# Strassen's scheme in the first product of the second MLP, with the planner's order kept to the end

## The chip, the cores and the metric

The kernel runs on one core of a Trainium2 chip. TensorE (PE) multiplies, VectorE (DVE), ScalarE (ACT) and GpSimd (POOL) work on elements, and SyncE (SP) issues most of the transfers, in the order of its queue. The metric is the device time of one execution in microseconds, the median of several.

## What is computed

An attention block feeds two MLPs one after the other; the tokens are 2304, the model width is 512 and the inner width 2048. The second MLP is the one that changes:

```python
def _moe2_ref(x, w_in, w_out, a, b):
    h = x @ w_in                       # 2304x512 by 512x2048: the first product
    h2 = h * h
    h3 = h2 * h
    P = a[0] + a[1] * h + a[2] * h2 + a[3] * h3
    Q = 1.0 + np.abs(b[0]) * np.abs(h) + np.abs(b[1]) * h2
    g = P / (Q + 1e-06)
    return (g @ w_out)                 # 2304x2048 by 2048x512: the second product
```

## The kernel before

**Split operands.** Every MLP operand is held as a rounded part and a rest (hi and lo, ACT's copy and a subtraction), and each block of a product is three matmuls into one PSUM bank: hi by hi, hi by lo, lo by hi.

**Tiles and units.** The second MLP goes through the tokens in six tiles of 384 (`T2`). Inner columns are taken 128 at a time, `ff` 0 to 15; a pair of tile and `ff` is a unit. `stage_a` makes the first product of a unit: four blocks of the model width, 12 matmuls of 128x384 (L1039 to L1041), into a bank `h` or `at`. `stage1`, `stage2` and `stage3` make the rational function of it on ACT, DVE and POOL and split the result into `gh` and `gl`. `stage_b`, three units later, makes the second product: three token blocks of 128, 9 matmuls of 128x512 (L1082 to L1084), into three banks `acc`. So a unit has 21 matmuls. `split_x` splits the tile's input, which `load_y` fetches.

**Weights.** During the last two tiles of the first MLP, `conv2_a` and `conv2_b` turn the weights of the second MLP from 64-bit into 32-bit floats and split them, one half of an `ff` at a time (half 0 is `w_in`, half 1 is `w_out`). They then stay in SBUF for all six tiles; those of `ff` 12 to 15 go out to HBM for a while and come back in `reload2`.

**Order.** A planner in the kernel (`plan`) simulates the engines with fixed costs and lists each engine's instructions in order. Its list is made binding for instructions that it starts before 600 us of its own clock (the last argument at the call); behind that the framework's scheduler keeps the written order, changed by priorities.

Of the kernel before, what the change touches and what calls it, by code (L numbers as in the profile page):

```python
# [8 lines left out]
F32 = mybir.dt.float32  # L9
# [50 lines left out]
SHARED = {("two", "wide"): 0.7, ("two", "thin"): 0.25, ("one", "wide"): 0.7, ("one", "thin"): 0.3,  # L60
          ("wide", "two"): 0.2, ("wide", "one"): 0.05, ("thin", "two"): 0.6, ("thin", "one"): 0.3}
HOLD, ROUNDS = 0.0, 6
DMA_RATE, DMA_LATENCY, LANES = 320e3, 1.9, 8


# [266 lines left out]
def moe_chain_kernel(ctx, tc, qk0, v0, qk, vv, s0, s, w1, w2, ab, out):  # L332
# [6 lines left out]
    l_d = [[dr.tile([128, 512], F32, name=f"l_d{t}_{i}") for i in range(2)] for t in range(NF)]  # L339
    w2_d = {(ff, half): [dr.tile([128, 512], F32, name=f"w2_d{ff}_{half}_{i}") for i in range(2)]  # L340
            for ff in range(FS, NF) for half in range(2)}
    y_d = {a: dr.tile([128, KD, b - a], F32, name=f"y_d{a}") for a, b in zip(CUTS, CUTS[1:])}

    def t_w(name, shape, dt):
# [42 lines left out]


    pt_h, pt_l, pt_p = [], [], []
    x_t = {}  # L390
    v_t = {}
    raw_t = {}
# [280 lines left out]
    def t1(p):  # L673
        if p.pv_plain:
            if not pt_p:
                pt_p.append(sb.tile([128, 2, 960], F32, name="pt"))
# [148 lines left out]
    n = 0  # L825
# [107 lines left out]
        if T == 0:  # L933
            li_t[1, ff, half] = l

    c2_open = []

    def conv2_a(ff, half):
        c2_open.append((ff, half, conv_t(1, ff, half)))

    def conv2_b():
        ff, half, t = c2_open.pop(0)
        if ff >= FS:
            hi, lo = (tmp_tile("PA", 3, (128, 512), F32R) for _ in range(2))
        else:
            hi, lo = home2(ff, half)
        last = {i.engine: i for i in traced()}
        k0 = len(nc.cur_bb.bb.instructions)
        conv_hl(t, hi, lo)
        queue_behind({nc.scalar.engine: last[nc.scalar.engine]}, k0)  # L950
        if ff >= FS:
            for d, t in zip(w2_d[ff, half], (hi, lo)):
                nc.sync.dma_start(out=d, in_=f(t))
        else:
            w2_t[ff, half] = (hi, lo)

    def home2(ff, half):
        if ff >= 14:
            return t_l("w2h", [128, 512], F32R), t_l("w2l", [128, 512], F32R)
        if ff < 2 and ff not in w2_t:  # L960
            t = t_j("w2", [128, 2, 1024], F32R)
            w2_t[ff] = (t[:, 0], t[:, 1])
        if ff not in w2_t:
            al = t_q if ff < 5 else t_v if ff < 6 else t_w
            w2_t[ff] = (al("w2h", [128, 1024], F32R), al("w2l", [128, 1024], F32R))
        return tuple(t[:, half * 512:(half + 1) * 512] for t in w2_t[ff])

    def reload2(ff):
        for half in range(2):
# [57 lines left out]
    def stage_a_(u):  # L1027
        ph, T, ff = u
        bk = bank(hsel(ph, T, ff))
        n = TILES[ph][T][1]  # L1030
        h = bk[:, 0:n]
        if ph == 0:
            wh, wl = w1_t[ff][:, 0:512], li_t.pop((T, ff, 0))
        else:
            wh, wl = w2_t[ff, 0]
        for k in range(KD):
            xh, xl = xs_t[ph, T, k]
            cs = slice(k * 128, (k + 1) * 128)
            nc.tensor.matmul(h, wh[:, cs], xh, start=(k == 0), stop=False)  # L1039
# [48 lines left out]
    def evacuate(ph, T, acc):  # L1088
# [42 lines left out]
    def stage1_(u):  # L1131
# [23 lines left out]
    def stage2(u):  # L1155
        ph, T, ff = u
        if ph == 0:
            return
        a, t, w = e_t[u]
        c = 1.0 + 1.0e-6  # L1160
# [5 lines left out]
        e_t[u] = t  # L1166

    def stage3(u):
        with early(P_ST3):
# [13 lines left out]
    if True:  # L1183
# [76 lines left out]
        units += [(ph, T, ff) for ph in range(2) for T in range(2 - 2 * ph, 6) for ff in range(NF)]  # L1260
        NU = len(units)
        T1A = [(1, ff) for ff in range(HF)]
        c2 = [(ff, half) for r in (range(6), range(FS, NF), range(6, FS)) for ff in r for half in range(2)]
        c2_done, c2_load = [0], [0]

        def load2_to(n):
# [32 lines left out]
            return bank("at")  # L1299

        open_acc(0, 0)
        for i in range(NU + LAGS[1]):
            at_bank[0] = second_bank if i < HF + LAGS[0] else at_only
            u = units[i] if i < NU else None
            region[0] = 0 if i < 32 else 1 if i < 96 else 2
            if u is not None:
# [4 lines left out]
                gap(i, 0)  # L1311
                stage1(u)
                with ahead(C2_OFF):
                    while c2_open:
                        conv2_b()
# [29 lines left out]
            if u is not None:  # L1345
# [5 lines left out]
                if 0 < t4 <= 20:  # L1351
                    conv2_to(t4)
                elif t4 > 20:
                    ready = 6 + (t4 - 18) // 2
                    conv2_to(min(2 * (NF - FS + ready), t4, 32))
                if t4 >= 34 and t4 % 2 == 0 and FS + (t4 - 34) // 2 < NF:
                    reload2(FS + (t4 - 34) // 2)
                if ph == 0 and T == 3 and ff == 8:
                    nc.sync.dma_start(out=abt, in_=ab)
                    nc.vector.memset(qc, 1.0 + 1.0e-6)  # L1360
# [4 lines left out]
                if ph == 1 and ff == 5 and T + 1 < 6:  # L1365
                    load_y(T + 1)
# [62 lines left out]
```

## Time and profile before

| | |
|---|---|
| median of three runs | 1037.35 us (1037.16 to 1037.57) |
| span of the profiled execution | 1033.6 us; the trace gives no other time of that execution |
| busy share of the span | PE 98%, ACT 77%, DVE 76%, POOL 43% |
| granted TensorE clock | 1.00 in all slices, which is 2.4 GHz |
| second MLP on PE | from 615.72 us to about 1029.4 us |

A matmul's time from start to end includes what overlaps with its neighbours, so the price of one is the distance from its start to the next one's. Busy times of the other engines are unions.

### The profile page before, as it was taken

How to read it: one execution, taken by the hardware profiler on the slowest of the kernel's cores; microseconds unless marked ns; L12 is line 12 of the kernel's file. 1: busy time of each engine (PE TensorE's matmuls, PEld its weight loads, DVE VectorE, ACT ScalarE, POOL GpSimd, SP SyncE). 2: the span in 40 equal slices, each digit the busy share in tenths (PEclk: the TensorE clock that was granted, in tenths of full speed). 3: DMA queues.
4: the chain of work that ended last, by engine and by line, in shares of the span. 5: the costliest groups of instructions: out<-in, count | busy, mean ns of one | idle time of the engine just before them, and what ended most of it. 6: DMA issues, size and time to landing. Idle time of an engine off the chain costs nothing.

```text
span 1033.6 us, 17441 instructions
## 1 busy us (share of the span) xinstructions
PE 1011.0 (98%) x5684; PEld 917.0 (89%) x5684; DVE 785.7 (76%) x1826; ACT 791.2 (77%) x1661; POOL 448.1 (43%) x491
## 2 busy tenths in 40 slices
PE   6999999999999999999999999999999999999998
PEld 5889999889998888988999999989999999999996
DVE  5788986887987888787675887687686766877765
ACT  5998878877987777766566558778887887877875
POOL 2757664412221122223435765445444454444542
PEclk9999999999999999999999999999999999999999
DMA  9877576665564644436779855010010110100100
GB/s 249 296 241 254 186 222 195 207 187 151 161 196 131 200 147 142 139 97 215 237 228 323 303 153 189 1 31 32 1 62 1 31 31 2 56 6 1 31 1 31
DMA packets 67946, 138.66 MB, mean 134 GB/s; under 512 B 8336, under 2 KB 21456, under 8 KB 67856
## 3 DMA queue, kind: packets, MB, share of 16 engines
q1 hardware_dynamic: 65312, 133.39, 40.7%
q10 hardware_dynamic: 2544, 4.16, 1.6%
q8 instruction: 45, 0.74, 0.3%
q14 instruction: 45, 0.37, 0.1%
HBM read 110.82 MB, written 22.61 MB: 129 GB/s over the span
## 4 chain that ended last, share of the span: by engine, by line
PE 76%; DVE 9%; ACT 5%; DMA 4%; POOL 4%; issue 3%; SPq 1%; POOLq 0%; DVEq 0%; ACTq 0%
PE h L1039 7%; PE h L1040 7%; PE h L1041 7%; PE at L754 6%; PE acc L1082 5%; PE acc L1084 5%; PE acc L1083 5%; PE acc L1077 4%; PE acc L1075 4%; PE acc L1076 4%; PE at L1039 3%; PE at L1040 3%; PE at L1041 3%; PE at L614 3%; PE at L615 2%
## 5 line engine op out<-in xcount | busy, mean ns | idle before, releaser
L607 POOL TENSOR_SCALAR PA<-PA,stat 128x384 f32<-128x384 f32 (+3 forms) x112 | 72.9, 657 | 165.1 <-DVE stat L606 65.7
L1039 PE MATMUL h<-xs,w1h 128*128 128x448 f32 (+1 forms) x360 | 122.8, 342 | 1.6 <-DVE e L1141 1.5
L1040 PE MATMUL h<-xs,w1h 128*128 128x448 f32 (+1 forms) x360 | 122.6, 341 | 0.0
L1041 PE MATMUL h<-xs,w1l 128*128 128x448 f32 (+1 forms) x360 | 122.3, 340 | 0.0
L1076 PE MATMUL acc<-gl,w1h 128*128 128x448 f32 (+1 forms) x352 | 118.8, 339 | 1.2 <-POOL gl L1179 1.2
L1077 PE MATMUL acc<-gh,w1l 128*128 128x448 f32 (+1 forms) x352 | 118.8, 340 | 0.4 <-DMA w1l<-l_d 0.3
L1075 PE MATMUL acc<-gh,w1h 128*128 128x448 f32 (+1 forms) x352 | 118.4, 340 | 0.0
L1179 POOL TENSOR_TENSOR gl<-PA,gh 128x384 fp32r<-128x384 f32 x95 | 97.1, 1022 | 7.3 <-ACT gh L1177 5.0
L1082 PE MATMUL acc<-w2h,gh 128*128 128x512 f32 x252 | 99.6, 395 | 0.1
L1084 PE MATMUL acc<-w2h,gl 128*128 128x512 f32 x252 | 99.3, 394 | 0.0
L1083 PE MATMUL acc<-w2l,gh 128*128 128x512 f32 x252 | 99.2, 394 | 0.0
L1150 POOL TENSOR_TENSOR tc<-tc,e 128x384 f32<-128x384 f32 x47 | 51.2, 1089 | 97.5 <-ACT tc L1148 97.5
L604 ACT ACTIVATE PA<-PA,stat 128x384 f32<-128x384 f32 (+3 forms) x112 | 63.9, 571 | 16.4 <-DVE stat L587 14.3
L1039 PEld LDWEIGHTS h<-xs,w1h 128*128 128x128 f32 x360 | 67.9, 189 | 5.7 <-DVE e L1141 2.4
L1040 PEld LDWEIGHTS h<-xs,w1h 128*128 128x128 f32 x360 | 67.8, 188 | 3.7 <-DVE xs L1009 0.4
L1041 PEld LDWEIGHTS h<-xs,w1l 128*128 128x128 f32 x360 | 67.8, 189 | 3.2
L1076 PEld LDWEIGHTS acc<-gl,w1h 128*128 128x128 f32 x352 | 66.1, 189 | 4.6 <-POOL gl L1179 1.4
L1077 PEld LDWEIGHTS acc<-gh,w1l 128*128 128x128 f32 x352 | 66.1, 189 | 3.9 <-DMA w1l<-l_d 0.5
L1137 ACT ACTIVATE e<-h 128x448 f32<-128x448 f32 (+1 forms) x90 | 43.4, 483 | 33.5 <-PE h L1041 31.6
L1075 PEld LDWEIGHTS acc<-gh,w1h 128*128 128x128 f32 x352 | 66.1, 189 | 3.2
L1177 ACT ACTIVATE gh<-PA 128x384 fp32r<-128x384 f32 x96 | 50.4, 525 | 20.9 <-DVE PA L1165 17.7
L1163 DVE SCALAR_TENSOR_TENSOR tc<-tc,e 128x384 f32<-128x384 f32 x48 | 27.5, 574 | 51.0 <-ACT e L1162 47.9
(265 smaller groups left out, 3183.8 us busy)
## 6 DMA issues: line engine op xcount, KB each, us to landing
w1l<-l_d SPq DMA_DIRECT2D x138, 256.0 KB
raw<-in_w_dram SPq DMA_DIRECT2D x48, 512.0 KB
raw<-in_qk_dram SPq DMA_DIRECT2D x24, 384.0 KB
l_d<-w1l SPq DMA_DIRECT2D x32, 256.0 KB
raw64x<-in_w_dram SPq DMA_DIRECT2D x16, 512.0 KB
raw<-in_qk_dram SPq DMA_DIRECT2D x8, 576.0 KB
w_d<-PA SPq DMA_DIRECT2D x16, 256.0 KB
R<-in_vv_dram SPq DMA_DIRECT2D x12, 320.0 KB
```

The source lines that it names most:

```text
L604: nc.scalar.activation(pt[:, 0:n], pt[:, 0:n], AF.Exp, bias=mn, scale=-1.0, accum_out=stat[:, i, 1:2])
L607: nc.gpsimd.tensor_scalar(pt[:, 0:n], pt[:, 0:n], stat[:, i, 2:3], 1.0, op0=ALU.mult, op1=ALU.mult)
L1039: nc.tensor.matmul(h, wh[:, cs], xh, start=(k == 0), stop=False)
L1040: nc.tensor.matmul(h, wh[:, cs], xl, start=False, stop=False)
L1041: nc.tensor.matmul(h, wl[:, cs], xh, start=False, stop=(k == KD - 1))
L1075: nc.tensor.matmul(o, wh[:, cs], gh, start=first and not both, stop=False)
L1076: nc.tensor.matmul(o, wh[:, cs], gl, start=False, stop=False)
L1077: nc.tensor.matmul(o, wl[:, cs], gh, start=False, stop=last and (not both or m % 2 == 1))
L1082: nc.tensor.matmul(acc[m], gh[:, cs], wh, start=first, stop=False)
L1083: nc.tensor.matmul(acc[m], gh[:, cs], wl, start=False, stop=False)
L1084: nc.tensor.matmul(acc[m], gl[:, cs], wh, start=False, stop=last)
L1179: eng.tensor_tensor(gl, g, f(gh), op=ALU.subtract)
```

## The change

Tile sizes of the second MLP become 384, 512, 512, 512, 384. The two tiles of 384 keep the old units. The three of 512 work in four groups `q` each. A group is a product of 512 inner columns by 512 tokens: the weight `a` is cut into 2x2 blocks (256 of the inner columns by 256 of the model width, two separate pairs `p` of 128 columns) and the input `b` into 2x2 blocks (256 of the model width by 256 tokens). In place of the eight block products, seven "slots" are computed (`SLOTS`), some of them on sums and differences. A slot is 12 matmuls of 128x256 (L1336). Partial sums stay in their PSUM banks and further slots add to them; ACT copies three states of them to the SBUF tile `pt` (`save`), and DVE adds those copies back (`add`), so that four blocks of 256 inner columns by 256 tokens come out. Each goes through `act1`, `act2`, `act3` and `out_part`, whose two calls are 12 matmuls of 128x512 (L1274 to L1276).

The sums of weights are made once, in `sum_make` (four DVE operations of 128x256 for a pair of `ff`) and `sum_split` (two ACT copies, two POOL subtractions), during the conversion. All `w_in` operands go to HBM (`keep_a` and `sum_split`), and one transfer of 512 KB per slot brings them back, up to 12 slots ahead (`load_wa`). The sums of inputs are made for each tile (`operand_steps`: five DVE subtractions, seven splits on ACT and POOL). The order of the weight conversions changes. The planner's list is binding to the end.

```diff
-T2 = [(t * 384, 384) for t in range(6)]
+T2 = [(0, 384)] + [(384 + t * 512, 512) for t in range(3)] + [(1920, 384)]
+SLOTS = [("a11", "b11"), ("a12", "b21"), ("s2", "t2"), ("s1", "t1"), ("s3", "t3"), ("s4", "b22"), ("a22", "t4")]
+    def sum_make(q, p):
+        t0, t1, u = pairs[q, p]
+        a, b = slice(0, 256), slice(256, 512)
+        nc.vector.tensor_tensor(u[:, a], t1[:, a], t1[:, b], op=ALU.add)
+        nc.vector.tensor_tensor(u[:, b], t0[:, a], t1[:, a], op=ALU.subtract)
+        nc.vector.tensor_tensor(t0[:, a], u[:, a], t0[:, a], op=ALU.subtract)
+        nc.vector.tensor_tensor(t0[:, b], t0[:, b], t0[:, a], op=ALU.subtract)
...
+        nc.scalar.activation(g[:, :, 0], t, AF.Copy)
+        nc.gpsimd.tensor_tensor(g[:, :, 1], t, f(g[:, :, 0]), op=ALU.subtract)
...
+    def act2(bl):
+        r = bl.h
+        t, w, a = bl.g
+        nc.scalar.activation(a, w, AF.Ln, bias=qc)
+        nc.scalar.activation(r, a, AF.Exp, scale=-1.0)
+        nc.vector.scalar_tensor_tensor(w, w, QC, r, op0=ALU.add, op1=ALU.mult)
+        nc.vector.scalar_tensor_tensor(w, w, -2.0, r, op0=ALU.add, op1=ALU.mult)
+        nc.vector.scalar_tensor_tensor(t, t, nega[:, 0:1], w, op0=ALU.add, op1=ALU.mult)
...
+    def keep_a(ff):
+        q, p, i = ff // 4, ff // 2 % 2, ff % 2
+        dst = wa_d[q][i][:, p].rearrange("p (b h c) -> p b h c", b=2, h=2)
+        for h, t in enumerate(w2_t[ff, 0]):
+            nc.sync.dma_start(out=dst[:, :, h], in_=f(t).rearrange("p (b c) -> p b c", b=2))
+
+    def slot(T, q, a, b, o, first):
+        w, (xh, xl) = wa_t[T, q, a], ops_t[T, b]
+        for p in range(2):
+            for k in range(2):
+                cs = slice(k * 128, k * 128 + 128)
+                wh, wl = w[:, p, 0, cs], w[:, p, 1, cs]
+                for n, (x, z) in enumerate(((wh, xh), (wh, xl), (wl, xh))):
+                    nc.tensor.matmul(o[:, p * 256:p * 256 + 256], x, z[:, k], start=first and p == k == n == 0,
+                                     stop=(k, n) == (1, 2), skip_group_check=True)
+        used[0] += 1
+        load_wa(used[0] + WA_AHEAD)
...
+        def save(k, n):
+            return lambda: nc.scalar.activation(hbuf(n), st[k], AF.Copy)
+
+        def add(x, k, n, new=False):
+            def run():
+                bl[x].h = bank(tags["w"]) if new else st[k]
+                nc.vector.tensor_tensor(bl[x].h, st[k], hbuf(n), op=ALU.add)
+            return run
...
+        ev = [(1, mm(0, "z", True)), (1.1, save("z", 0)),
+              (2, mm(1, "y", True)), (2.1, add((0, 0), "y", 0)),
+              (3, mm(2, "z")), (3.1, save("z", 2)),
+              (4, mm(3, "v", True)), (4.1, save("v", 1)),
+              (5, mm(4, "z")), (5.1, add((1, 1), "z", 1, True)),
+              (6, mm(5, "v")), (6.1, add((0, 1), "v", 2)),
+              (7, mm(6, "z")), (7.1, direct)]
...
-    for line in plan(nc.cur_bb.bb.instructions, tied, 600.0):
+    for line in plan(nc.cur_bb.bb.instructions, tied, UNTIL):
```

**The order on PE in the middle of a tile.** Before, in a tile of 384 (`xs` and `yt` the input, `w2h` and `w2l` the weights):

```order
L1039 MATMUL h<-xs,w2h 128x384
L1082 MATMUL acc<-w2h,gh 128x512
L1040 MATMUL h<-xs,w2h 128x384
L1083 MATMUL acc<-w2l,gh 128x512
L1041 MATMUL h<-xs,w2l 128x384
L1084 MATMUL acc<-w2h,gl 128x512
```

Now, in the second of the tiles of 512 (`at` is the bank `z`, `h` the banks `y`, `v` and `w`; `xl` and `xs` the inputs, `wa` the slot's weights, `w2b` those of the second product):

```order
L1336 MATMUL at<-xl,wa 128x256 x12
L1274 MATMUL acc<-w2b,gh 128x512
L1275 MATMUL acc<-w2b,gh 128x512
L1276 MATMUL acc<-w2b,gl 128x512
...
L1336 MATMUL h<-xl,wa 128x256 x12
L1336 MATMUL at<-xl,wa 128x256 x12
L1274 MATMUL acc<-w2b,gh 128x512
L1275 MATMUL acc<-w2b,gh 128x512
L1276 MATMUL acc<-w2b,gl 128x512
...
L1336 MATMUL h<-xs,wa 128x256 x12
```

The two products no longer alternate one by one: slots of 12 stand between stretches of 6 or 12 matmuls of the second product, and the third slot, which adds to the bank of the first, follows the second directly.

**The order on PE where the first tile of 512 begins.** The part now, just ahead of its first second product (before, a tile's first units simply took up the same alternation):

```order
L1140 MATMUL acc<-w2b,gl 128x512 x3
L1336 MATMUL h<-xs,wa 128x256 x8
L1336 MATMUL at<-xl,wa 128x256 x5
L1336 MATMUL at<-xs,wa 128x256
L1336 MATMUL at<-xl,wa 128x256
L1336 MATMUL at<-xs,wa 128x256 x4
L1336 MATMUL h<-xs,wa 128x256
L1336 MATMUL at<-xs,wa 128x256 x7
L1336 MATMUL h<-xs,wa 128x256
L1336 MATMUL at<-xl,wa 128x256
L1336 MATMUL h<-xs,wa 128x256 x10
L1336 MATMUL at<-xl,wa 128x256 x11
```

Behind the last matmuls of the tile of 384 (L1140) only slots stand for a while, and those of the second group (`at<-xl`) are drawn in among those of the first.

**The order on POOL in the last tile of the first MLP** (`gl` is the unit's own work, `raw` and `w2l` or `w2a` the conversion). Before:

```order
L1179 TENSOR_TENSOR gl<-e,gh 128x448
L904 TENSOR_SCALAR raw64x<-raw64x 128x512
L912 TENSOR_TENSOR w2l<-tc,w2h 128x512
L1179 TENSOR_TENSOR gl<-e,gh 128x448
```

Now (`pt` are the sums' rests):

```order
L1393 TENSOR_TENSOR gl<-e,gh 128x448
L914 TENSOR_SCALAR raw64x<-raw64x 128x512
L922 TENSOR_TENSOR w2a<-tc,w2a 128x512 x2
L1393 TENSOR_TENSOR gl<-e,gh 128x448
L998 TENSOR_TENSOR pt<-tc,pt 128x2x256 x2
L922 TENSOR_TENSOR w2a<-tc,w2a 128x512
L1393 TENSOR_TENSOR gl<-e,gh 128x448
```

Between two units' `gl` there are now up to three operations of the conversion and the sums, and the last of these stand in the first tile of the second MLP.

## Rows read from the trace of the kernel before

**Rows 1.** The page's busy times of the engines.

```profile
PE 1011.0 (98%) x5684; PEld 917.0 (89%) x5684; DVE 785.7 (76%) x1826; ACT 791.2 (77%) x1661; POOL 448.1 (43%) x491
```

**Rows 2.** Busy time of each engine in stretches: clock, DMA share, GB/s last.

```profile
core 0: us, PE busy (x) PEld busy (x) DVE busy (x) ACT busy (x) POOL busy (x), PEclk, DMA share, GB/s
160.00:180.00 20.00, 19.86 (x163) 19.24 (x163) 13.84 (x40) 16.29 (x40) 9.24 (x11) 1.00 0.58 184
260.00:280.00 20.00, 20.00 (x123) 18.54 (x122) 18.06 (x66) 18.22 (x49) 4.87 (x10) 1.00 0.54 158
280.00:300.00 20.00, 20.00 (x119) 18.25 (x118) 18.14 (x60) 18.00 (x44) 5.25 (x10) 1.00 0.63 185
560.00:580.00 20.00, 20.00 (x100) 18.46 (x99) 12.02 (x15) 11.25 (x20) 15.01 (x13) 1.00 0.99 345
600.00:620.00 20.00, 20.00 (x102) 18.63 (x101) 17.41 (x20) 11.82 (x22) 12.35 (x10) 1.00 0.46 132
680.00:700.00 20.00, 18.86 (x93) 16.55 (x93) 15.51 (x27) 15.87 (x32) 8.56 (x8) 1.00 0.14 40
700.00:1000.00 300.00, 300.00 (x1506) 271.30 (x1505) 216.78 (x378) 242.92 (x454) 148.34 (x144) 1.00 0.07 22
```

**Rows 3.** What PE waited for from 480 us on: total, times, longest.

```profile
PE h L1040 <- DVE xs L1013: 1.1, 1, 1.1
PE h L1039 <- DVE PA L1152: 0.2, 1, 0.2
```

**Rows 4.** Timeline of PE, first and last of 22 matmuls of 128x512.

```profile
1021.34 0.39 PE L1083 MATMUL acc<-w2l,gh 128*128 128x512 f32 x1
...
1026.21 0.39 PE L1083 MATMUL acc<-w2l,gh 128*128 128x512 f32 x1
```

**Rows 5.** Timeline of PE, first and last of 31 matmuls of 128x256.

```profile
88.40 0.28 PE L1039 MATMUL h<-xs,w1h 128*128 128x256 f32 x1
...
91.92 0.28 PE L1077 MATMUL acc<-gh,w1l 128*128 128x256 f32 x1
```

**Rows 6.** Weight loads in the stretch of rows 5: busy, mean ns.

```profile
L1039 PEld LDWEIGHTS h<-xs,w1h 128*128 128x128 f32 x7 | 1.3, 189 | 0.0
```

**Rows 7.** Groups by line and shape from 560 us on: busy, mean ns.

```profile
L1179 POOL TENSOR_TENSOR gl<-PA,gh 128x384 fp32r<-128x384 f32 x95 | 97.1, 1022 | 7.3 <-ACT gh L1177 5.0 <-issue 2.3
...
L1177 ACT ACTIVATE gh<-PA 128x384 fp32r<-128x384 f32 x96 | 50.4, 525 | 20.9 <-DVE PA L1165 17.7
...
L1151 DVE TENSOR_TENSOR PA<-PA,h 128x384 f32<-128x384 f32 x50 | 27.3, 547 | 2.2 <-ACT PA L1149 2.2
...
L912 POOL TENSOR_TENSOR w2l<-tc,w2h 128x512 fp32r<-128x512 f32 x12 | 16.9, 1408 | 3.0 <-ACT w2h L911 3.0
...
L1013 DVE TENSOR_TENSOR xs<-yt,xs 128x384 fp32r<-128x384 f32 x18 | 16.1, 917 | 0.0
...
L911 ACT ACTIVATE w2h<-tc 128x512 fp32r<-128x512 f32 x12 | 7.4, 620 | 0.0
...
L1111 ACT ACTIVATE yb<-acc 128x512 f32<-128x512 f32 x11 | 6.4, 586 | 1.2 <-PE acc L1084 1.2
...
L1113 DVE COPY yb<-acc 128x512 f32<-128x512 f32 x6 | 4.1, 686 | 1.3 <-PE acc L1084 1.3
```

**Rows 8.** Timeline of one late unit, its first ACT and its last POOL operation.

```profile
1012.24 0.49 ACT L1147 ACTIVATE e<-at 128x384 f32<-128x384 f32 x1 [0.24 <-PE at L1041]
...
1019.12 1.04 POOL L1179 TENSOR_TENSOR gl<-PA,gh 128x384 fp32r<-128x384 f32 x1
```

**Rows 9.** Timeline, the last matmul of the kernel.

```profile
1029.04 0.39 PE L1084 MATMUL acc<-w2h,gl 128*128 128x512 f32 x1
```

More of the change, by code (lines that the diff above doesn't have):

```diff
@@ L341, in moe_chain_kernel @@
             for ff in range(FS, NF) for half in range(2)}
+    wa_d = [[dr.tile([128, 2, 1024], F32, name=f"wa_d{q}_{d}") for d in range(4)] for q in range(4)]
     y_d = {a: dr.tile([128, KD, b - a], F32, name=f"y_d{a}") for a, b in zip(CUTS, CUTS[1:])}
@@ L389, in moe_chain_kernel @@
     pt_h, pt_l, pt_p = [], [], []
+    keep = {}
     x_t = {}
@@ L675, in t1 @@
             if not pt_p:
-                pt_p.append(sb.tile([128, 2, 960], F32, name="pt"))
+                keep["pt"] = sb.tile([128, 2, 1024], F32, name="pt")
+                pt_p.append(keep["pt"][:, :, 0:960])
             p.pt = (pt_p[0][:, p.h % 2],)
@@ L1003, in split_x_ @@
             hi, lo = (y_t[T][:, KD + i] for i in range(2))
+        elif (ph, T) == (1, TAIL):
+            hi, lo = (t_l("xl", [128, 512], F32R)[:, 0:n] for _ in range(2))
         else:
@@ new lines, in moe_chain_kernel, with out_part @@
+    acc2 = {}
+    def out_part(bl, p):
+        gh, gl = bl.g
+        wh, wl = w2_t[4 * bl.q + 2 * p + bl.i, 1]
+        first, last = (bl.T, bl.j) not in acc2, bl.ends and p == 1
+        if first:
+            acc2[bl.T, bl.j] = [bank("acc") for _ in range(2)]
+        acc = acc2[bl.T, bl.j]
+        for m in range(2):
+            cs = slice(p * 256 + m * 128, p * 256 + m * 128 + 128)
+            nc.tensor.matmul(acc[m], gh[:, cs], wh, start=first, stop=False)
+            nc.tensor.matmul(acc[m], gh[:, cs], wl, start=False, stop=False)
+            nc.tensor.matmul(acc[m], gl[:, cs], wh, start=False, stop=last)
+        if last:
+            yb = sb.tile([128, 2, 512], F32, tag="R", bufs=2, name="yb")
+            nc.scalar.activation(yb[:, 0], acc[0], AF.Copy)
+            nc.vector.tensor_copy(yb[:, 1], acc[1])
+            for m in range(2):
+                for b, s0, w, o in tokens(T2[bl.T][0] + bl.j * 256 + m * 128, 128):
+                    nc.sync.dma_start(out=out[b * S + s0:b * S + s0 + w, :], in_=yb[o:o + w, m])
@@ new lines, in hbuf, with group, mm, run @@
+    def hbuf(n):
+        return keep["pt"].rearrange("p a b -> p (a b)")[:, n * 512:n * 512 + 512]
+    def group(T, q, at, events):
+        st = {}
+        bl = {(i, j): Block(T, q, i, j) for i in range(2) for j in range(2)}
+        tags = dict(zip("zyvw", ("at", "h", "h", "h")))
+        def mm(k, to, first=False):
+            def run():
+                if first:
+                    st[to] = bank(tags[to])
+                slot(T, q, *SLOTS[k], st[to], first)
+            return run
+        def save(k, n):
+            return lambda: nc.scalar.activation(hbuf(n), st[k], AF.Copy)
+        def add(x, k, n, new=False):
+            def run():
+                bl[x].h = bank(tags["w"]) if new else st[k]
+                nc.vector.tensor_tensor(bl[x].h, st[k], hbuf(n), op=ALU.add)
+            return run
+        def direct():
+            bl[1, 0].h = st["z"]
+        ev = [(1, mm(0, "z", True)), (1.1, save("z", 0)),
[5 more added lines that the diff above has]
+              (7, mm(6, "z")), (7.1, direct)]
+        events += [(at + t, fn) for t, fn in ev]
+        for x, t in (((0, 0), 2.2), ((1, 1), 5.2), ((0, 1), 6.2), ((1, 0), 7.2)):
+            for n, (d, fn) in enumerate(((0, act1), (1.75, act2), (3.5, act3))):
+                events.append((at + t + d, lambda x=x, fn=fn: fn(bl[x])))
+            for p in range(2):
+                events.append((at + t + 5.25 + 0.875 * p, lambda x=x, p=p: out_part(bl[x], p)))
@@ L1301, in moe_chain_kernel @@
         open_acc(0, 0)
-        for i in range(NU + LAGS[1]):
+        for i in range(NU):
             at_bank[0] = second_bank if i < HF + LAGS[0] else at_only
@@ L1313, in moe_chain_kernel @@
                 with ahead(C2_OFF):
-                    while c2_open:
-                        conv2_b()
+                    conv2_b()
                 if ph == 0 and T == 0:
@@ L1364, in moe_chain_kernel, with operand, tail_a @@
                     load_y(0)
-                if ph == 1 and ff == 5 and T + 1 < 6:
-                    load_y(T + 1)
-    for line in plan(nc.cur_bb.bb.instructions, tied, 600.0):
+                if ph == 1:
+                    keep_a(ff)
+                    if ff == 2:
+                        load_y(1)
+                    if ff >= 9:
+                        load_wa(min(ff - 8, 7))
+        events = [(0.3, lambda: stage2(units[NU - 1])), (0.4, lambda: stage3(units[NU - 2])), (1.7, lambda: stage3(units[NU - 1]))]
+        for n in range(3):
+            events.append((1.4 + 1.5 * n, lambda n=n: stage_b(units[NU - 3 + n])))
+        steps = {}
+        def operand(T, n):
+            if T not in steps:
+                steps[T] = operand_steps(T)
+            steps[T][n]()
+        for T in range(1, TAIL):
+            at = 28 * (T - 1)
+            for q in range(4):
+                group(T, q, at + 7 * q, events)
+            events.append((at + 9.3, lambda T=T: load_y(T + 1)))
+            for n in range(7):
+                events.append(((at - 5.7 + n if T > 1 else 0.01 + 0.05 * n if n < 2 else 0.5 + 0.9 * n), lambda T=T, n=n: operand(T, n)))
+        at = 28 * (TAIL - 1) + 1
+        def tail_a(u):
+            stage_a(u)
+            used[0] += u[2] % 4 == 3 and 4
+            load_wa(used[0] + WA_AHEAD)
+        for k in range(KD):
+            events.append((at - 4 + k, lambda k=k: split_x(1, TAIL, k)))
+        for ff in range(NF):
+            u = (1, TAIL, ff)
+            for t, fn in ((0, tail_a), (0.1, stage1), (1.5, stage2), (2.9, stage3), (4.3, stage_b)):
+                events.append((at + 1.4 * ff + t, lambda u=u, fn=fn: fn(u)))
+        region[0] = 2
+        for _, fn in sorted(events, key=lambda e: e[0]):
+            fn()
+    for line in plan(nc.cur_bb.bb.instructions, tied, UNTIL):
         for prev, i in zip(line, line[1:]):
```

139 lines of the change are left out of this document (115 added, 24 removed).

## Prediction

> **What bounds the kernel now.** I began with the page's busy times [rows 1]: PE is busy for 98% of the span, ACT and DVE for three quarters. An average hides stages, so the table by stretches came next [rows 2]. From 700 to 1000 us, the middle of the second MLP, PE is busy for 300.00 of 300 us at a granted clock of 1.00 (2.4 GHz), while DVE has 216.78 and ACT 242.92. The list of waits [rows 3] confirms it: from 480 us to the end PE waited 1.3 us in all, of which 1.1 us lie at one place, where the second tile's input was split late (the stretch 680 to 700 with 18.86). So in the part that changes, time is the number of matmuls by their price, and only what shortens PE's own work or makes it wait will show.
>
> **What PE saves.** Three prices are needed. A matmul of 128x512 costs (1026.21 - 1021.34) / 21 = 0.232 us from start to start [rows 4]. The stretch 700 to 1000 has 1506 matmuls, 0.1992 us on average, so a unit of 21 takes 4.183 us, and its 12 of 128x384 cost (4.183 - 9 x 0.232) / 12 = 0.175 us [rows 2]. For 128x256, the shape of the slots, the second MLP has no row, but the first one's small tiles do: (91.92 - 88.40) / 30 = 0.1173 us, with another weight block for each matmul, as in a slot [rows 5].
>
> The 1536 tokens of the three large tiles were 64 units: 64 x 4.183 = 267.7 us. Now they are 12 groups, each with 7 x 12 = 84 matmuls of 128x256 and, for four blocks, 48 of 128x512: 84 x 0.1173 + 48 x 0.232 = 21.0 us, in all 251.9 us. That is **15.8 us less**. The other two tiles keep their units. As the dearer end of the slot's price I take the 20 us most crowded with such matmuls, attention's among them: 20 / 163 = 0.1227 us [rows 2], which makes the groups 257.3 us and the saving 10.4 us. I use 0.1173, since that is the same shape in an unbroken run.
>
> Against this stands the weight load of each matmul. Its row shows 189 ns [rows 6], more than the matmul's 117 ns; yet the matmuls in that same stretch follow each other at 117 ns, so loads overlap even here. The Trainium skill, "TensorE: Matmul & The Clock Gate", section "LDWEIGHTS (loading the stationary operand)", puts a load at columns / 1.2 ns, some 107 ns for 128 columns: as long as 256 columns take to stream, so that a slot would have no slack where the old shapes had some. By that page a load that is not overlapped would about double a slot's matmuls, an estimate of 84 x 0.107 = 9 us a group; the spacing of the run decides against it.
>
> **What the other engines get.** A unit now takes 242.92 / 71.7 = 3.39 us of ACT, 3.02 of DVE and 2.07 of POOL, with 71.7 units in the stretch [rows 2]. A block is 512 columns wide in place of 384; rows at both widths give factors [rows 7]: ACT's copy 620 / 525 = 1.18, DVE reading PSUM 686 / 547 = 1.25 (another operation, but the nearest), POOL 1408 / 1022 = 1.38.
> - ACT, a group: four blocks 4 x 4.00, three `save` at 0.586, and a quarter of seven operand splits at 0.62: 18.8 us of 21.0.
> - DVE: 4 x 3.79, three `add` at 0.686, and a quarter of five subtractions at 0.917 x 1.25: 18.7 us.
> - POOL: 4 x 2.85 and a quarter of seven splits at 1.41: 13.9 us.
>
> All are below PE's 21.0, two of them at about 90%. The nearest stretch with such a load under a list of the planner is 260 to 300 us: DVE 18.1 and ACT 18.1 of 20, and PE 20.00 [rows 2]. So dense work on the helpers need not stall PE. But the groups add a wait that units don't have: a bank is added to again only after ACT has copied it. In the order of the middle of a tile, six matmuls of the second product and the second slot lie between the first and third slot, 6 x 0.232 + 12 x 0.117 = 2.8 us, for a copy of 0.59 us and what stands ahead of it on ACT. Behind a late third slot wait all of PE's queue, and the `add` of the next block. The bounds are 0 (260 to 300 us) and one wait of 1.1 us a group as in [rows 3], 13.2 us; I take 1.5 us for all twelve groups, near the first.
>
> **Entry.** The first tile of 512 has no second product of its own until its first block is through. A late unit needs from its first ACT operation to the end of its last POOL operation 1019.12 + 1.04 - 1012.24 = 7.9 us [rows 8]; at 512 columns, by 1.3 (the mean of the three factors), 10.3 us. Between the end of the second slot and the first such matmul, PE's order has 87 slot matmuls and 18 of the old tile: 10.2 + 4.2 = 14.4 us. POOL, however, has four operand splits of 1.41 us ahead of the block's last subtraction: 10.3 + 5.6 = 15.9 us. So a wait of about **2 us** (0, if the splits fall into idle time; 6 by the rival on transfers below).
>
> **Conversion.** The sums add 16 POOL subtractions of 1.41 us, 16 ACT copies of 0.62 and 32 short DVE operations, about 23, 10 and 13 to 20 us, to the stretch from 520 to 690 us. POOL is busy 15.0 of 20 us at 560 [rows 2], so it fills up there, and by its new order hands the rest to the first tile of the second MLP, where a unit takes half of it (148.34 of 300). PE's order is the same as before up to the second MLP, and a unit's `gl` has three units, 12 us or more, before it is needed. I put 0.5 us here (0 to 4, a few waits like that of [rows 3]).
>
> **The sum.** -15.8 + 1.5 + 2 + 0.5 = -11.8 us. The tail is the old one, the last matmul at 1029.04 in a span of 1033.6 [rows 9]; the longer list binds its order, which already left PE almost no wait, so I give it nothing. The span becomes 1021.8 us. The span before is 1033.6 and the runs' median 1037.35, so 3.75 us lie around it, and I carry them over: **1025.5 us**.
>
> **Rivals.**
> - *Transfers at the entry.* Between the first MLP's last weights and the seventh slot load, SP's order now has 63 transfers with 21.4 MB (most of `keep_a`, the reloads, the last sums, the input, seven loads). In 16 units, 67 us, that is 320 GB/s; the most that a stretch shows is 345 at a DMA share of 0.99, and 280 to 300 us, at 185 for a share of 0.63, scales to 293 [rows 2]. At 293 they need 73 us, 6 us too many. For it: the queue is in order, and a slot load waits for a free buffer and holds up the rest. Against it: the seventh load is needed only at the seventh slot. Price some 6 us: 1031.5.
> - *Waits in the groups* (the other side). If each group loses one wait of 1.1 us, 13.2 in place of 1.5 us, the time is 1037, no gain. If two, one at the third and one at the fifth slot, it is about 1051. The point from which it decides is (267.7 - 251.9 - 2.5) / 12 = 1.1 us a group. For it: ACT and DVE at 90%, strict queues, and waits of 1 us in 20 in stretches like 160 to 180 are seldom but there (19.86). Against it: 260 to 300 us.
> - *Slots paced by weight loads.* At 0.189 a matmul: 1008 x 0.072 = 72 us more, about 1098; the run of [rows 5] speaks against it.
>
> **Chances.** As summed, 1021.5 to 1029.5: 0.58. Transfers or a bad entry, 1029.5 to 1035: 0.17. Waits that eat the gain, 1035 to 1039.5: 0.07; that make it slower: 0.13. Weight loads 0.01. Still faster, since the list also closes the old 1.3 us: 0.04. A measurement of this kernel can tell about 0.2%, 2 us: faster 0.79, same 0.07, slower 0.14. The range 1021.5 to 1037 takes in the first two and half of the third, 0.79 to 0.8 of the chance.
>
> **What the profile will show.** Right: 20 us in the large tiles hold some 126 matmuls with PE at 20.0, each 12 of a slot 1.41 us apart; ACT and DVE near 18 of 20; the last matmul near 1017. Waits of PE for DVE, ACT or POOL near the first slots of about 2 us, and none regular after. Wrong: PE waits that come back once a group at the third, fifth or seventh slot, with ACT (`save`) or DVE as releaser; matmuls of 128x256 further apart than 0.12 us; PE waiting for `wa` from HBM; PE waits before 690 us for POOL's `gl`.

## The result and the profile after

The change makes the kernel slower: 1048.88 us (median of 4 runs, 1048.24 to 1049.92) beside 1037.26 us of the kernel before on the same chip, a ratio of 1.0116 with a 95% interval of 1.0101 to 1.0130. Forecast was 1025.5 us, so 23.4 us are to be explained. The profiled execution has a span of 1046.6 us.

The page's busy times, beside [rows 1]:

```profile
PE 1005.5 (96%) x5924; PEld 902.2 (86%) x5924; DVE 846.5 (81%) x1815; ACT 785.6 (75%) x1620; POOL 506.7 (48%) x496
```

PE's busy time is only 5.5 us lower, in a span that is 13 us longer. Busy time misleads here: a matmul ahead of a wait counts to its end, past the moment at which the next could have started, and a stretch at the lower clock counts in full. I therefore also counted from start to start: each matmul at the prices of the prediction (and 0.2035 us for 128x448, from the dense 540 to 600 us), and as lost what is left of the distance to the next one. From 600 us on the matmuls cost 426.4 us before and 410.3 now, 16.1 less, and the lost time rises from 2.5 to 32.1 us.

Where PE waits is told by the table by stretches, with the columns of [rows 2]:

```profile
600.00:620.00 20.00, 16.64 (x78) 14.06 (x77) 18.40 (x20) 10.76 (x21) 14.82 (x12) 1.00 0.77 260
620.00:640.00 20.00, 17.87 (x84) 16.70 (x85) 18.78 (x25) 9.80 (x19) 14.96 (x13) 0.91 0.80 283
640.00:660.00 20.00, 15.44 (x77) 13.25 (x77) 18.43 (x26) 12.63 (x25) 12.90 (x11) 1.00 0.85 274
660.00:680.00 20.00, 18.51 (x87) 15.05 (x86) 16.07 (x26) 15.07 (x30) 14.42 (x12) 1.00 1.03 371
680.00:700.00 20.00, 19.81 (x97) 17.02 (x96) 18.19 (x26) 15.56 (x30) 14.08 (x12) 1.00 0.66 242
700.00:720.00 20.00, 17.96 (x110) 15.40 (x109) 18.32 (x26) 16.25 (x31) 15.03 (x12) 1.00 0.56 184
760.00:780.00 20.00, 19.67 (x123) 17.32 (x122) 16.92 (x23) 16.31 (x29) 12.35 (x9) 1.00 0.55 178
780.00:800.00 20.00, 18.76 (x120) 16.70 (x120) 19.31 (x24) 15.27 (x27) 15.41 (x11) 1.00 0.42 142
800.00:820.00 20.00, 20.00 (x127) 17.79 (x126) 16.73 (x25) 17.18 (x30) 12.68 (x10) 1.00 0.80 265
940.00:960.00 20.00, 20.00 (x130) 18.05 (x128) 16.07 (x24) 15.97 (x29) 10.29 (x8) 1.00 0.52 171
1020.00:1040.00 20.00, 17.29 (x79) 13.58 (x77) 15.11 (x24) 12.57 (x26) 7.25 (x8) 1.00 0.01 1
```

Read it from the bottom of the large tiles upward. At 800 and 940 us PE is dense with 127 and 130 matmuls, where 126 were forecast: the Strassen groups do what they should. The loss lies elsewhere. From 600 to 680 us, the end of the first MLP and the first tile of the second, where PE had waited for next to nothing before [rows 2, 3], it lacks 3.36 + 2.13 + 4.56 + 1.49 = 11.5 us, with DVE at 16 to 19 of 20. The entry to the large tiles (680:720) lacks 2.2 us, a turn between them (760:800) 1.6, and the tail 2.7. From start to start the lost time is 16.6 us from 600 to 680 (before 0.5), 5.8 from 680 to 740 (before 1.4), 5.2 from 740 to 960 (before 0.0) and 4.5 behind 1020 (before 0.5). The five longest rows of PE's waits from 480 us on, against the 1.3 us of [rows 3]:

```profile
PE acc L1138 <- ACT gh L1391: 6.3, 7, 1.9
PE h L1095 <- DVE e L1197: 5.3, 4, 3.1
PE h L1095 <- DVE PA L1209: 3.0, 4, 1.7
PE acc L1276 <- POOL gl L1260: 2.1, 4, 1.2
PE acc L1140 <- POOL gl L1393: 1.5, 5, 0.4
```

L1197 is DVE's one operation in a unit of the first MLP's last tile: it frees the unit's bank. L1209 does so in the first tile of the second MLP. Both rows fall between 600 and 680 us. The `gh` of L1138 belongs to the second MLP's tiles of 384: 1.9 us of its 6.3 lie from 640 to 660, some 2 at the entry and 2.4 in the tail. DVE's own queue shows why L1197 is late (timeline: start, duration, line, tiles):

```profile
599.51 1.52 DVE L915 TENSOR_SCALAR tc<-raw 128x512 int32<-128x512 int32 x1
601.07 1.67 DVE L916 SCALAR_TENSOR_TENSOR tc<-raw,tc 128x512 int32<-128x512 int32 x1
602.77 0.69 DVE L917 SCALAR_TENSOR_TENSOR tc<-raw,tc 128x512 int32<-128x512 int32 x1
603.38 0.62 DVE L1197 SCALAR_TENSOR_TENSOR e<-h,e 128x448 f32<-128x448 f32 x1
603.91 0.42 DVE L915 TENSOR_SCALAR tc<-raw64x 128x512 int32<-128x512 int32 x1
604.36 1.69 DVE L916 SCALAR_TENSOR_TENSOR tc<-raw64x,tc 128x512 int32<-128x512 int32 x1
606.09 1.53 DVE L917 SCALAR_TENSOR_TENSOR tc<-raw64x,tc 128x512 int32<-128x512 int32 x1
607.72 0.68 DVE L986 TENSOR_TENSOR tc<-tc 128x256 f32<-128x256 f32 x1
608.32 0.86 DVE L987 TENSOR_TENSOR tc<-tc 128x256 f32<-128x256 f32 x1
609.11 0.61 DVE L1197 SCALAR_TENSOR_TENSOR e<-h,e 128x448 f32<-128x448 f32 x1
```

and POOL's beside it:

```profile
599.26 2.93 POOL L998 TENSOR_TENSOR pt<-tc,pt 128x512 fp32r<-128x512 f32 x2
604.20 1.30 POOL L922 TENSOR_TENSOR w2a<-tc,w2a 128x512 fp32r<-128x512 f32 x1 [2.01 <-ACT w2a L921]
605.46 1.61 POOL L1393 TENSOR_TENSOR gl<-e,gh 128x448 fp32r<-128x448 f32 x1
...
608.88 1.43 POOL L922 TENSOR_TENSOR w2a<-tc,w2a 128x512 fp32r<-128x512 f32 x1
```

Between two L1197 lie 5.7 us, while the 24 matmuls of a unit of the first MLP take PE 24 x 20.00 / 100 = 4.8 us [rows 2]. The queue is without a gap, and the same operation has two lengths: L915 takes 0.42 us at 603.91, when POOL stands idle until 604.20, and 1.52 at 599.51, when POOL is in its L998. L1197, which reads the bank in PSUM, keeps its 0.61 at 609.11 too, beside POOL's L922.

### The profile page after: what moved, and what is told of

Its sections match the earlier page's. It is cut to its first block, busy times and chain, and to the rows that moved or that the text cites. A ratio compares the mean times of both kernels' runs of the same rounds, so it can differ in the third digit from the quotient of the medians.

```text
span 1046.6 us, 18293 instructions
## 1 busy us (share of the span) xinstructions
PE 1005.5 (96%) x5924; PEld 902.2 (86%) x5924; DVE 846.5 (81%) x1815; ACT 785.6 (75%) x1620; POOL 506.7 (48%) x496
## 5 line engine op out<-in xcount | busy, mean ns | idle before, releaser
L1260 POOL TENSOR_TENSOR gl<-PA,gh 128x512 fp32r<-128x512 f32 x48 | 63.7, 1328 | 70.1 <-issue 57.3
L1393 POOL TENSOR_TENSOR gl<-e,gh 128x256 fp32r<-128x256 f32 (+1 forms) x48 | 47.6, 992 | 29.9 <-ACT gh L1391 24.7
L1276 PE MATMUL acc<-w2b,gl 128*128 128x512 f32 x144 | 55.5, 397 | 2.0 <-POOL gl L1260 2.0
L1274 PE MATMUL acc<-w2b,gh 128*128 128x512 f32 x144 | 56.8, 394 | 0.0
L1275 PE MATMUL acc<-w2b,gh 128*128 128x512 f32 x144 | 56.7, 394 | 0.0
L596 DVE CUSTOM_DVE_ANT_0 PA<-at,mask 128x384 f32<-128x384 f32 (+3 forms) x100 | 50.4, 518 | 5.9 <-PE at L624 3.9
L623 PE MATMUL at<-ht 128*128 128x512 f32 (+3 forms) x156 | 53.5, 348 | 1.1 <-DVE stat L604 0.8
```

The costliest lines, as they stand in the source:

```text
L1260: nc.gpsimd.tensor_tensor(gl, bl.g, f(gh), op=ALU.subtract)
L1274: nc.tensor.matmul(acc[m], gh[:, cs], wh, start=first, stop=False)
L1275: nc.tensor.matmul(acc[m], gh[:, cs], wl, start=False, stop=False)
L1276: nc.tensor.matmul(acc[m], gl[:, cs], wh, start=False, stop=last)
```

## The experiments

The theory (A): the sums and the conversions fill DVE at the end of the first MLP, since their operations get two to three times longer beside POOL's. Rivals: (B) the work would fit, but the planner's list, now bound to the end, orders it badly; (C) transfers. Ratios are to the kernel before, on the same chip. Every edit of the program makes the planner order it anew, so a difference of a few us between two runs need not be the work of the edit alone.

**e1, without the sums.** Edit: `sum_make` and `sum_split` gone, and

```diff
             d, e = DUOS[a]
+            d %= 2
```

> Leaves out the sums of the weight quarters (32 DVE operations, 16 ACT copies, 16 POOL subtractions, 16 transfers); the slots that need them read other quarters of the same size, so PE's matmuls and the loads are unchanged and only the values differ. Theory A (the sums fill DVE, and through POOL slow it, from 600 to 700 us): the stretches 600:700 lose under 4 us of PE's 100 in place of 11.7, and the time falls by 10 to 14 us, to 1035 to 1039. Theory B (the work fits, but the list of the planner, which now binds to the end, puts conversions ahead of the units' own operations): the conversions stay where they are, so at least half of the loss stays: 1042 to 1047. Theory C (transfers of 620 to 680, DMA share 0.80 to 1.03): 4 of 21 MB go, so about 1046.

Measured 1036.23 us, 0.9999 (0.9989 to 1.0008). The time is A's; those of B and C are missed. One bound of A is missed too: 600:700 lacks 5.2 us, not under 4, since the entry is now worse (4.8 us at 680, where the changed kernel lacks 0.2). The table by stretches shows the end of the first MLP dense:

```profile
600.00:620.00 20.00, 20.00 (x102) 18.64 (x101) 16.39 (x19) 12.77 (x24) 12.94 (x11) 1.00 0.98 344
640.00:660.00 20.00, 20.00 (x103) 18.12 (x102) 13.49 (x22) 14.02 (x28) 9.41 (x9) 1.00 0.91 304
680.00:700.00 20.00, 15.21 (x72) 12.03 (x71) 19.00 (x23) 12.56 (x24) 14.71 (x11) 0.94 0.32 106
```

The DMA share rose to 0.98 with PE dense: transfers are not it.

**e2, the list up to 600 us.** Edit: `UNTIL = 600.0`.

> The planner's list binds only instructions that it starts before 600 us, as before the change; behind that the program's priorities decide, which put conversions 20 places behind the units' work. All work is the same. Theory B: the stall of 600:700 goes, time 1033 to 1040 if the groups do as well by priorities, and PE's waits for the unit's softplus sum at L1197 and gh at L1391 vanish. Theory A: DVE's work between 600 and 700 is as much as before, so the stall stays or moves into the second MLP's first tile: 1045 to 1052. In both the last 20 us show how much of the tail's 3 us of waits is the list's.

Measured 1077.62 us, 1.0396 (1.0381 to 1.0412): worse than either theory gave. PE has 15.36 of 20 at 600 us and 11.59 at 640, so priorities don't cure the stall, and 16.98 and 15.70 at 740 and 800, so they are worse for the groups. That is one other order; it does not show that no order would do. Its last 20 us held one wait of 0.4 us: the tail's waits are the list's.

**e3, the kernel before with the list to the end.** Edit: `tied, 600.0` becomes `tied, 2000.0`.

> The kernel before, with its list bound to the end in place of 600 us; nothing else. Theory B expects a stall there too where the first MLP ends, and the time up by 4 us or more, 1041 or above. Theory A expects no more than 2 us either way (1035 to 1039.5), since without the sums DVE has 12 to 17 us of 20 in that stretch.

Measured 1045.59 us, 1.0082 (1.0066 to 1.0097). Here B is right, and it was a blind spot: the long list alone costs the old kernel some 8 us. PE stays dense from 600 to 680, but waits at the turn to the second tile and in the tail. From its list of PE's waits from 480 us on:

```profile
PE h L1039 <- ACT xs L1012: 3.7, 1, 3.7
PE acc L1082 <- ACT gh L1177: 1.3, 2, 1.1
```

**e4, the sums' subtractions off POOL** (copies on ACT).

```diff
-        nc.gpsimd.tensor_tensor(g[:, :, 1], t, f(g[:, :, 0]), op=ALU.subtract)
+        nc.scalar.activation(g[:, :, 1], t, AF.Copy)
```

> The sums' 16 subtractions on POOL (L998) are replaced by 16 copies on ACT, so the low parts of the sums hold wrong values; DVE's 32 operations stay. If POOL's operations are what stretches DVE's (ops of 0.41 to 0.69 us that last 1.5 us beside POOL), DVE's busy in 600:660 falls from 55.6 to under 52 us and the time by 4 to 8 us, to 1041 to 1045. If DVE's own 32 operations are the load, POOL's part matters little: under 2 us.

Measured 1038.25 us, 1.0015 (1.0005 to 1.0025): taking 16 operations off POOL gives back 10 us of the 12 that leaving out the sums gives, more than expected. DVE's busy in 600:660 fell from 55.6 to 53.7 us, less than expected.

**e5, the tail by priorities.** Edit: the instructions emitted from the seventh unit of the last tile on are left out of the list.

> The planner's list no longer binds what is emitted from the seventh unit of the last tile on; there the program's priorities decide, as before the change. All else as changed. Theory: in the changed kernel the list leaves three units' second products to the end, where PE's starts lie 1.4, 0.8, 1.2, 0.8 and 0.9 us apart in place of 0.23, some 4 us lost; by priorities these gaps close, and the time is 1044 to 1046. Rival: the last units' chains (ACT, DVE, POOL) are too long however they are ordered: 1048 or more.

Measured 1045.90 us, 1.0089 (1.0072 to 1.0106), about 2.8 us less: the list's price in the tail.

**e6, the sums' subtractions on DVE.** Edit: in the line of e4, `nc.vector` in place of `nc.gpsimd`.

> The sums' 16 subtractions (L998) run on DVE in place of POOL; everything is computed. If POOL's operations stretch DVE's (both wait for each other), DVE gains more than the 16 x 0.69 us = 11 us that it takes on: DVE's busy in 600:660 stays below the 55.6 us of the changed kernel, and the time falls by 3 to 9 us, 1040 to 1046. If DVE is simply full, its new work makes it worse: 1052 or more.

Measured 1046.39 us, 1.0096 (1.0081 to 1.0111). The fuller engine got more work and the kernel became no slower, but some 2 us faster (the two intervals just overlap), which "DVE is simply full" excludes. But the gain is below the forecast's, and DVE's busy rose to 57.1 us in 600:660: it is full as well (19.84 of 20 at 620).

**e7, the lighter conversion and the tail of e5.**

```diff
-            nc.gpsimd.tensor_scalar(hf, hf, 2.0 ** -112, 1.0, op0=ALU.mult, op1=ALU.mult)
-            nc.vector.tensor_scalar(ti, hw, 3, None, op0=ALU.logical_shift_left)
-            nc.vector.scalar_tensor_tensor(ti, hw, -2147483648, ti, ...)
-            nc.vector.scalar_tensor_tensor(ti, lw, 29, ti, ...)
+        nc.vector.tensor_scalar(ti, lw, 29, None, op0=ALU.logical_shift_right)
+        nc.scalar.activation(hf, hf, AF.Prelu, scale=2.0 ** -112, alpha=-(2.0 ** 32))
+        nc.vector.scalar_tensor_tensor(ti, hw, 3, ti, op0=ALU.logical_shift_left, op1=ALU.bitwise_or)
```

> The tail as in the run above, and the conversion of the second MLP's weights done as the first MLP's: the scaling is an ACT operation (Prelu) in place of POOL's L914, and two DVE operations in place of three. POOL loses 32 operations of 0.8 to 1.1 us, DVE 32 of 0.7 to 1.7 us, ACT gains 32 of about 0.7 us. If the crowd on DVE and POOL up to 680 us is the cause, PE is at 19.5 or more of 20 in each stretch from 600 to 680, and the time is 1032 to 1037 with the tail's 4 us. If the list's order is the cause, under half of that: 1040 to 1045.

Measured 1034.62 us, 0.9981 (0.9971 to 0.9990), as expected in time, but not in every stretch: PE still has 18.52 at 600 and 15.82 at 640.

**e8, dearer prices for the planner.** Edit: the figures in `SHARED` and POOL's line in `Step`.

> As the run above, and the planner is told dearer prices: POOL's subtraction of 512 columns 1.40 us in place of 1.27, its strided scaling 1.10 in place of 0.64, and a DVE operation beside a POOL operation longer by 1.3 of the overlap in place of 0.7. If the entry's waits (685 to 720, about 6 us, PE waiting for gh of the old tile's last units) come from an order that the planner's too cheap prices made, they shrink by 2 us or more, and the time is 2 us or more below the run above. If the entry's work is itself too much for DVE and POOL, the times agree within 2 us.

Measured 1044.36 us, 1.0071 (1.0053 to 1.0088): 10 us worse than e7. Neither theory expected it, and the loss lies elsewhere: from 0 to 540 us PE gets through 3206 matmuls, in e7 through 3255, and 49 matmuls of 0.2 us are 10 us. The widest gap is in a part that the change does not touch, where attention ends:

```profile
460.00:480.00 20.00, 15.14 (x63) 11.61 (x62) 11.36 (x39) 10.36 (x25) 2.87 (x5) 0.71 0.41 137
```

From 540 us on the two lose as much, 19.2 us from start to start beside 19.7 of e7, and at the entry (680:740) PE lacks 3.5 us in both. So the dearer prices made the order of the first half worse, and did not mend the entry.

**e9, conversions earlier, by way of HBM.** Edit, the core:

```diff
-        if ff >= FS:
+        if ff >= FS or half == 0:
             hi, lo = (tmp_tile("PA", 3, (128, 512), F32R) for _ in range(2))
...
+                if 21 <= t4 < 21 + FS:
+                    reload0(t4 - 21)
```

> As e7, and the first-product half of every weight block goes straight to HBM when it is converted and is loaded back into the buffer that the first MLP frees, so that no conversion waits for a buffer of the first MLP and the sums are made earlier; the copies of the second MLP's first tile (keep_a) fall away. The first sums stand 5 units of the first MLP earlier on DVE, the last 2. If the crowd at 600 to 680 us is what is left of the loss (PE lacks 6 us of 80 there in e7), it shrinks by 3 us or more, time 1029 to 1032. If the transfers set the pace of the conversions (DMA share 0.95 from 540 to 600), the conversions don't move and the time is within 2 us of e7.

Measured 1041.62 us, 1.0058 (1.0041 to 1.0075), outside both bounds. The edit brought a wait of its own. The `PA` buffers are also those of the second MLP's units, and now a conversion holds them until its transfer has landed, at a DMA share of 1.02 and 1.05 (620:660). PE's first wait, and one of ACT's, from 600 to 660 us:

```profile
PE h L1109 <- DVE PA L1223: 10.1, 3, 5.2
```

```profile
ACT PA L1220 <- DMA wa_d<-PA: 2.5, 1, 2.5
```

**e10, e7 with the sums' subtractions on DVE.**

> As e7, and the sums' 16 subtractions run on DVE in place of POOL, as in e6. If POOL's share of the shared work is the larger part of the rest, another 2 us, as from e6: 1031 to 1034. If DVE is now the fuller one, 1035 or more.

Measured **1028.79 us**, 0.9926 (0.9909 to 0.9943), better than expected, the best version that computes everything, and faster than both kernels. What took 2 us off the changed kernel in e6 takes 5.7 off e7, whose conversion has a third fewer DVE operations. Its table by stretches:

```profile
600.00:620.00 20.00, 20.00 (x102) 18.62 (x101) 17.49 (x25) 14.48 (x28) 8.00 (x7) 1.00 0.92 330
640.00:660.00 20.00, 18.48 (x91) 15.88 (x90) 18.77 (x31) 16.46 (x32) 10.34 (x9) 1.00 1.06 365
680.00:700.00 20.00, 18.74 (x100) 15.27 (x99) 19.86 (x26) 14.02 (x27) 13.12 (x10) 1.00 0.58 194
760.00:780.00 20.00, 18.04 (x108) 15.39 (x107) 18.77 (x24) 14.05 (x25) 14.28 (x11) 1.00 0.45 146
```

At 600 DVE is busier than in e7 (17.49, there 16.78) and POOL less (8.00, there 14.99), and PE is dense. What is left lies at 640, at the entry and at the turn.

**e11, e7 with the operand splits' subtractions off POOL** (copies on ACT, in `split`).

> As e7, but the 21 subtractions on POOL that split the operands of the three large tiles (seven a tile, 512 columns) are copies on ACT, so the low parts hold wrong values. If these subtractions, crowded with the old tile's last units, make the waits at the entry (680:740: PE lacks 3.5 us in e7) and at the turns between large tiles (760:800: 1.2 us, two such places), most of these 6 us go: 1029 to 1032. If the entry waits for something else (transfers, or the order), the time is within 1.5 us of e7.

Measured 1031.70 us, 0.9957 (0.9943 to 0.9972), 2.5 us below e7. This understates it, since by 540 us this order is behind e7 by 18 matmuls (3237 and 3255), 3.6 us; from there on the lost time falls from 19.7 to 12.9 us. PE lacks 0.7 us at 680:740 and 0.2 at 760:800. So POOL's subtractions are behind the waits at the entry and the turns. That they act there through DVE is likely (at 680:700 it does 29 operations in 17.51 us, in e7 26 in 19.53), but not separated from POOL's own queue.

**e12, e9 and e10 together.**

> The edits of e9 and e10 together. If they add up, 1027 to 1031; if both take away the same wait, the better of the two within 1.5 us.

Measured 1046.28 us, 1.0094 (1.0079 to 1.0109): a miss, with e9's wait grown to 12.8 us.

**e13, the kernel before with the lighter conversion.**

> The kernel before with the lighter conversion alone (Prelu on ACT, two DVE operations in place of three). If the lighter conversion pays only where the sums crowd DVE and POOL, nothing changes, since PE waited 1.3 us from 480 us on: 1035 to 1039. If it is worth time of its own, the gain of e10 is not the change's: 1033 or less.

Measured 1034.76 us, 0.9976 (0.9967 to 0.9986), between the two: some 2.5 us of its own. Its profiled span, 1033.7 us, is that of before (1033.6), so no stretch shows where; that execution lies at the upper end of its times (1035.45 us, of 1033.47 to 1035.61), while the kernel before has spans from 1032.8 to 1037.6 on that chip. If the two add up, the rest of e10's gain, 0.9926 against 0.9976 or 5 us, comes from the changed kernel.

**e14, e1 with the lighter conversion and the free tail.**

> e1 (sums left out, the slots read other quarters) with the lighter conversion and the free tail. It shows what is left when the first MLP's end is not crowded at all. If the sums were the whole of what e10 still lacks there (1.5 us at 640:660), the time is 1025 to 1028. If entry and turns hold more, 1028 to 1031.

Measured 1031.49 us, 0.9949 (0.9931 to 0.9967): just above both bounds and, with less work, slower than e10. PE is at 20.00 from 600 to 680 and lacks 7.2 us at the entry (14.88 and 17.89 in 680:720), where e10 lacks 2. So the sums are not what is left. A likely reason is that each kernel's list orders the entry anew, worth several us either way; no run isolates it.

**e15, e10 with the operand splits' subtractions off POOL, as in e11.**

> e10 with the operand splits' subtractions as copies on ACT, as in e11 (low parts hold wrong values). If the entry and the turns between the large tiles are what e10 still lacks to the prediction (3.3 us), 1024.5 to 1027; if something else, 1028 or more.

Measured 1024.59 us, 0.9883 (0.9861 to 0.9905), as expected. In its table by stretches entry and turn are dense or nearly so:

```profile
680.00:700.00 20.00, 20.00 (x120) 17.87 (x119) 17.89 (x27) 18.73 (x37) 10.40 (x9) 1.00 0.73 230
760.00:780.00 20.00, 19.79 (x123) 17.46 (x122) 15.94 (x25) 19.57 (x35) 9.77 (x8) 1.00 0.54 164
```

Its span of 1021.5 us is that of the forecast (1021.8), and its last matmul starts at 1016.18 (forecast: near 1017). Part of that is luck: this kernel leaves low parts of the operands wrong, so it is no version to use, and it has the lighter conversion, which the forecast did not.

## Why the prediction was wrong

**What PE saves** was right. In the dense part a slot stands as forecast, 12 matmuls from 845.12 to 846.53, 1.41 us, in the timeline of the changed kernel:

```profile
845.12 1.58 PE L1336 MATMUL at<-xs,wa 128*128 128x256 f32 x12
846.53 0.40 PE L1274 MATMUL acc<-w2b,gh 128*128 128x512 f32 x1
```

Counted from start to start PE saves 16.1 us (forecast 15.8). The rival on weight loads falls with it, and no row of PE's waits names a transfer. **What the other engines get** was somewhat high (DVE 15.5 to 16.7 and ACT 15.7 to 17.2 of 20 in the dense stretches, where 18 were forecast), and the waits in the groups, turns included, cost 5.2 us from 740 to 960 (1.5 were taken), half of them at the first turn. The rival that ended slower had the sign, but not the place: PE does not wait once a group.

**Conversion is the step that failed.** It took 0.5 us (0 to 4) because the sums' work was added engine by engine: POOL 23 us, DVE 13 to 20, and POOL was watched as the one that fills up. From 600 to 680 us 16 us more are lost than before. The sums' price on POOL was right (L998: 24.3 us), that on DVE too low (6.7 + 5.9 + 7.0 + 8.4 = 28.0 us from 540 to 690), and the argument beside them wrong in two places. First, operations of the two engines lengthen each other; POOL's L998 too takes 1.28 us at its shortest and 1.75 at its longest. The trace of the kernel before had shown it for one operation of the conversion:

```profile
606.04 1.37 DVE L905 TENSOR_SCALAR tc<-raw64x 128x512 int32<-128x512 int32 x1 [1.70 <-POOL w2l L912]
...
610.30 0.41 DVE L905 TENSOR_SCALAR tc<-raw 128x512 int32<-128x512 int32 x1
```

```profile
605.97 1.15 POOL L1179 TENSOR_TENSOR gl<-e,gh 128x448 fp32r<-128x448 f32 x1
```

Two of the four groups, by form, in the changed kernel from 540 to 690 us (busy us, mean ns, idle before):

```profile
L989 DVE TENSOR_TENSOR tc<-tc 128x256 f32<-128x256 f32 x8 | 8.4, 1051 | 0.2
L988 DVE TENSOR_TENSOR tc<-tc 128x256 f32<-128x256 f32 x8 | 7.0, 870 | 0.2
```

Set against POOL's timeline, these operations last 0.42 us where POOL is idle for most of them, and 0.92 to 1.33 us in the median of each line where it is not; L915 0.41 and 1.37, L916 0.68 and 1.53. Second, "a unit's `gl` has three units, 12 us or more, before it is needed" looked at the wrong end of the unit: from 597 to 621 us each of DVE's L1197 stands behind five operations of the conversion and the sums, and it frees the bank, so PE waits for its next bank. The prediction had looked for waits before 690 us at POOL's `gl`; they came, but at DVE. Taking the sums away (e1), or only their part on POOL (e4), or lightening the conversion (e7 against e5) each gives 10 us or more back. Without the sums (e1), the time lost from 540 us to the first slot falls from 18.9 to 2.9 us.

**Entry** had the right work, but another wait and size. The wait of 2 us was to come where the first block's second product needs its result; there PE lost 0.2 us, and 0.6 at a slot that waited for `pt`. Some 2 us were lost earlier, at the second products of the old tile's last units. From 680 to 740 us 4.3 us more are lost than before. Without POOL's part of the operand splits the time falls by 2.5 us (e11 against e7) and 4.5 (e15 against e10), turns included, and the time lost from 540 us on by 6.8 and 6.2.

**The sum**, where it gives the tail nothing, missed 2.8 us (e5). That its order "already left PE almost no wait" was said of a list that ended at 600 us; bound to the end it costs even the old kernel 8 us (e3). The 3.75 us around the span, carried over, did no harm to a difference of medians, but in later runs a time of the kernel before lies 2.2 us above its own span: the profiled execution lay below the median.

From start to start the account closes: -16.1 for PE's work, +16.1 from 600 to 680, +4.3 at the entry, +5.2 in the large tiles and +4.0 in the tail are 13.5 us, and the last matmul starts 13.5 us later than before. Forecast were -15.8, 0.5, 2, 1.5 and 0. The runs retrace it in ratios: 1.0116 as changed, 1.0089 with the free tail, 0.9926 with the lighter conversion and the sums on DVE (0.0024 of it is the conversion's own, e13), 0.9883 without POOL's operand subtractions, which no longer computes everything. The forecast was 1025.5 / 1037.35 = 0.9886. What stays open: why one list is several us better than another at the entry (e10, e14), and where the old kernel gains from the lighter conversion.

## What to carry to other kernels

Where DVE and POOL both get new elementwise work on SBUF, don't add up each engine's time alone: price an operation at its length beside the other engine, and ask which operation of the critical chain stands behind it in the queue. DVE at 12 to 17 of 20 us had no free room here, since its queue is in order and its operations could double. Work that is taken off the crowded pair (a scaling on ACT, a subtraction from POOL to DVE) gave more here than any new order of the same work that was tried. And a longer time does not tell where it was lost: e8 lost its 10 us in a part that the edit was not meant for.

## What was not expected of the hardware

A DVE operation beside a POOL `tensor_tensor` is not slowed a little, but held: `tensor_scalar` of 128x512 goes from 0.41 to 1.52 us, though it has one tensor input. Who starts first decides. Of the conversion's and the sums' DVE operations from 540 to 690 us, 13 start before the POOL operation beside them and keep their length within 5%; 38 start while one runs, and all are longer, 1.1 to 3.7 times, and end 0.28 us (those of 0.41 to 0.42 us alone) or 0.55 us (those of 0.68) after POOL's. Seven beside POOL's L914 alone, a `tensor_scalar`, take 1.6 to 2.2 times as long. In the changed kernel (shortest, median and longest, ns):

```profile
L915 DVE TENSOR_SCALAR tc<-raw x16: 410/427/1522, 410.3 to 639.9; 128x512 int32<-128x512 int32 x16
L989 DVE TENSOR_TENSOR tc<-tc x8: 424/1224/1520, 542.3 to 657.9; 128x256 f32<-128x256 f32 x8
```

L1197, with one input in PSUM, keeps its time: 0.61 to 0.62 us in all 16 of that stretch, beside POOL or not. The Trainium skill, "GPSIMD Engine Reference", section "1. Specifications", says that POOL's SBUF interfaces are shared with DVE, with contention for DVE instructions with two SBUF inputs or in a two-port mode. The rows agree for the operations with two SBUF inputs and show a size; in which mode the `tensor_scalar` ran, no run here shows.

PE's stalls also cost beyond themselves. Its longest wait, 3.1 us, ended at 621.9 us, and the mean granted clock was 0.91 in 620:640; if the rest is at the lower of the two levels, 1.2 GHz, that is 0.09 x 20 / 0.5 = 3.6 us at half speed. The timeline agrees: from 622.8 to 626.2 us matmuls of 128x384 and 128x448 start 0.32 and 0.37 us behind one another, 1.83 times the distance before and after, which costs 1.5 us.
